# A fourth buffer of H, outputs through lent buffers, and a new written-out order

## The chip, the cores and the metric

The kernel runs on one core of one Trainium2 chip. Such a core has a matrix engine (TensorE, PE in the profile), three engines for elementwise work (VectorE or DVE, ScalarE or ACT, GpSimd or POOL) and a queue (SyncE, SP) from which this kernel issues all its transfers. Each engine runs its own instructions in the order in which they stand in the program, and waits at an instruction until what it needs is there. The metric is the device time of one execution in microseconds; for the kernel before it is the median of three runs.

## The reference

There are four batches of 6272 steps with 256 channels. First a gated recurrence runs along the steps:

```python
sig = 1.0 / (1.0 + np.exp(-f_logit))
f = lower_bound + (1.0 - lower_bound) * sig
i = 1.0 - f
for t in range(S):
    h = f[:, t] * h + i[:, t] * x[:, t]
    y[:, t] = h
```

Its output goes through a projection into three parts of 256 channels. The middle part is convolved, circularly and over all 6272 steps, with a filter for each channel; the result is multiplied by the first and the third part and projected once more:

```python
proj = x @ w_proj                        # x is the y of the recurrence
x1, x2, x3 = the three parts of proj
X2 = np.fft.rfft(x2, n=S, axis=1)
H = np.fft.rfft(filter_fft, n=S, axis=0)[None, :, :]
x2_conv = np.fft.irfft(X2 * H, n=S, axis=1)
out = (x1 * x2_conv * x3) @ w_out
```

## The kernel before

The transform over 6272 = 128 x 49 steps is done as two shorter ones, by matrix products: 128 points, then 49 with a twist (as 98 real rows). The channels are worked in 16 units (`u`) of 16 channels each.

For each batch the steps of the program are these; the words in brackets are the names that the text uses and the lines at which they stand.

- The recurrence (`hgrn`, L318). 13 chunks of 512 steps, the last of 128. For each chunk logits and x are loaded (`load`, L331, 512 KB each), ScalarE takes the sigmoid (`sig`, L334), GpSimd multiplies it with x (`u`, L336), TensorE transposes both (`su`, L348), ScalarE or VectorE makes the gate (`f`, L361 or L363), and VectorE runs the scan (`scan`, L369) into HA. The first 3072 results of each half are repeated behind the last, by GpSimd, ScalarE or a transfer (`wrap`, the helper at L283 to L295).
- The middle projection (`phase_p`, L704). `P` (L713), 13 groups of up to eight products, needs the scan of the whole batch; each group is copied to X2 (`x2`, through the helper, L283 or L288).
- The transform (`phase_f1`, `mini`, `unit`). `F1` (L726) and its copy to A; `F2` (L785); the product with the filter's spectrum H into PP, either by VectorE straight from the matrix engine's results (L806) or by a copy and GpSimd (L815); the way back `I2` (L825) and its copy to Th. H was made once, in a preparation at the start, and lies in HBM; each unit loads its 512 KB (`spectrum_load`, L763) into one of `NH` buffers. The least recently used buffer is taken, and since the units go up in one batch and down in the next, the last `NH` units of a batch find their H in place in the next. With three buffers that makes 55 loads.
- The gate (`gate`, L384): the first and third projections (`x13`, L397) and their product z (L418 by VectorE, L427 by GpSimd).
- The output (`phase_o`, L852). 13 chunks `g`. For each: the second half of the way back (`I1`, L865), needing Th of all units; the product with z into ys (`y`, L871); the output projection (`proj`, L883); the copy of its result into an output buffer (`o`, helper, L285 or L290); the store from there (`store`, L894, 512 KB).

The output buffers are three of their own (`NO = 3`, names `osb`) and four lent ones for chunks 3 to 6: the two buffers PP and two halves of A. A lent buffer is free once the last unit of the batch is done with it, and has to be free again for the first units of the next.

All this is recorded first as a list of steps with what each reads and writes (`Plan.op`), and then issued in the order of a table, `ORDER`, that was made outside of the kernel. An entry names the step, the engine that runs it (where two or three can) and the PSUM bank. The order on each engine and on SP's queue is the table's order, so a later batch's recurrence stands between the earlier batch's steps wherever the table puts it. Each step carries a cost, which only the maker of the table used; transfers carry beside it a `margin` of one microsecond:

```python
op("H", {"SP": 0.46}, lambda e: nc.sync.dma_start(...),
   r=[("H", u, i) for i in range(2)],
   w=[("Hu", h)] + ([("hs", h, a) for a in range(2)] if first else []),
   dma=1.7, lag=2.0, margin=MARGIN)
```

24 groups of four products of no use (`warm`, L599) can stand anywhere; they keep the matrix engine busy.

Of the kernel before, what the change touches and what calls it, by code (L numbers as in the profile page):

```python
# [9 lines left out]
F32 = mybir.dt.float32  # L10
# [14 lines left out]
Q = 49  # L25
# [7 lines left out]
NH = 3  # L33
NO = 3
# [25 lines left out]
class Plan:  # L60
# [63 lines left out]
    "A+gD5gAAYABIACIAsQA0gA5gA1AAyQAgQAuQBDgBNgBXgBIgAhQBSgBhgArQBcgAeQAbQAoQA6ABrgAOYAPIAQAARIAzYA2QA4AA7SA9CA8CBmgA"  # L124
    "/YBAUBBEBCEBwgATIBEYBFWAUIAcSBHGBOYBPSBGGD6gA3ABJYBKUBLEBMMBYYEGgASABTYBRCBQCBZQBaIBbIBiYBUWBWGBjSBlCBkCBdYBeQBg"
    "ABfAAWIBsIBtSBuCBnIBoUBvCAVYAXYAYYAZYAaYBVOAdQBxIBpMByQBzABqMB3SB4KB0AB5QB6ID8AB+UB/MEIAB7YCASCBKD7gD9YCCYCHQESg"
    "EUAEHgB8UCIICDSCECCOWCPGB9MCJQCKIADgAEYD+SD/KEAKEegEgACQUCREECQAFgEDAEEICMWCNGEJYETgCLYCSYCXUAIACYMCZSCaKCeWAHAA"
    "KACTQCfOCUAAGgEfgEKUELMEMMCbYCcSCdCEqgEOWEPGErgCgQEQOEVYChACiYCnSCoCEhYEsACpUCFgCqMCGgE3gE2gCjQCkIEWSEXCEYKEaWEb"
    "GFDgEZgCwUCxEEcOEtYAJACrYCuQGJgCvACyYB1YEiUEjEFCgEmSFMgEnCCzQC0AEkME4AEuWDAUDBECsQCtAEoKEvOEySEzCC+UE5YFNgC5QFEA"
    "FFYEwOFWgALAC/MCVgC6IC3WC4GC7YDCYFXgDDUDEEE0KE6QE7IC8WC9OFOAFPYE8IE+SE/CFggFhgDOUDPEDQWFGUFAKFYAFZYFHEFIMDRGC2gF"  # L130
    "JQFKAFqgAMAE1YFLIDHSDICDJWDKODLYDSYFBYFrgFQUFRMFSMFTSF0gF1gFiAFjYFUCFVKDTQDUADMWDNGDWgFaQFdUF+gDZWFbAFcIFeMFfMF/"
    "gDXSFsAFtYC1gDaGDYCFkWDbYExYDgQF2AFnSF3YEdYEpYFlGFmODeUEFYERYE9YDhAFuQDFgFoCFpKMtgDfEDcWFxUM5gM4gFvAFwIDdGDiYFyE"
    "FzMDpSDqCF4WB2YDjQF5GF6ODkAANACWgF7SGIgCmgDnUMsgF8CDoMDrYDuQGAAGBYF9KEBYJdWJeXJfGDvADwUDxEDyYJgvJiWJkGClgGCQGDIG"
    "EIGFSDsUGGCGHKElYDtEMhgDzWD0GENYMuAMvYD3QGKgD4ID2gGhSGiKGRUGSEGfQGgIGbWGcGGLSGMKMggM6ADlgGPQGQAGjUGkEDVgGTWGUODG"
    "gGZSGaCJjQJloJmYMiAMjYGdUGeMGNSGOCM7YGXQGYAGVUGWMDmgJnSJpKJoTJqrJrYJsQJuAJtRGlUGmEJxQJzIGnWGoGGrSJvpGsKJwYGpUGqE"
    "D1gJyQJ2RJ4BJ0oGwWGtSGuKGyGG5UGvgG0uGzYJ3QJ7RJ5oJ6YJ9BHVSHWCG6YHBgJ1YG1YJ8WKAXKCHJ+uKBRHCSGxYKDBKEYHLWHNGG4gG9sG"
    "+YG7sG8YG2QHGqHKgHDYHECHTVHFYG3AKFSKGUKHCKIsKJYG/QHUFHdgJhYHOYHmgHMYKKSHAIHPuHQYKMCHvgHXTHHYHIVHYDHJFHZQHaAKLSKN"
    "qHeTKPVKQSKRFHirHjYKSCHbQHcIKOYHnWHfYHrGHRUHsYHSEKUSKVXIBQHgrH4gKWCHpuILgHqYKXvKYYICAHoYHhYHkUHlEHwSH0qH1YHyqHzY"
    "HxYIFQIGAIUgKTYIDWHtUKZTKbLH5QIEGHuEIHWIIGH7oH8YH9oH+YH2SIMUIJWIKOH6YKaQH3CIOEIdgKeSIPYKgCINYKcoKfRKhBIQsImgH/TI"
    "VWIWYIXuIRYIADMkQIeSIZGMlAMmIIgCMoUNEgNFgMpEMqMIaYISWITGJ/YIfYKjSKlCIvQIwAIhYIYYI5gIbWIcGInUIoYIiqIjYIrMIsYJCgIx"  # L140
    "QIyAIpsIqYIzSI0CMwWMxOM0QNQgNRgM1AKiYKkUKoVMyONGANHYM2II1SI2CJLgIkWIlGKmsKqFI3SI4KI7YI6QI+oI/YI8AI9YMnYItWIuGJEY"
    "KpSKrqKsYJDUJFEJGYJHsJIYM8QM9ANAWNcgNdgNBGM+IKtSKuTKvCKwrKxYJAUJNYKySNSANTYKzQK3RK0CNCOK1oK2YJBEK5BJMSJQCJRYNIWN"
    "MUJUgNogKdYJJQNpgKnYNJGJOqJPYJWYNNEJKANKONOMK4SK8TNeANfYNUWNYQNygJVUNVGK+DNzgK6qK7YNWOK9SK/qJXEJYYNZALAYLBTNaIJZ"
    "ELDDLCULEsLFYLGWLIGNqANrYMrgLHXLJvLLSLMTNgQNkUN9gLNCLOrLPYLKYJaYNhALQSNlELSCJSWJTGN0AN1YN8gLRTLVSLXCNiILWQLaRNsW"
    "LTrLcBLbTNmMNtGLYoLZYLdrLeYNvUOHgOGgNuOLUYNwENxMJbQJcAR9SR+TSADLkQLlINXYNjYLfWR/CN+ANDYN2UN5SORgOQgLgON6CN7KN/YL"
    "mQN3EN4MLnANPYNbYLogOIAOJYLhWLpSLqKSCQSEALuULvMLiGLjgOAQOBAOCIODSOagObgOECOFKLrWLzULsGL0MLtgOKQL4WOSAOTYMzYNnYOL"
    "AOMILwSL5OLxCLygM/AL1UL9QL+IL2EL3gONSOkgOlgOOCOPKOUWMCUOVGOWOOcAOdYL6QL7AL8gMDML/SMHQMIIMACMBgOXWOYGOZOOeUOhSVMg"
    "VNgOfEOgMM3AOmAOiCOjKMJQMKAMLgMEWOnYOoUOpEOqMOrQVZgVYgMRSOsAOtIVAgMFGMGgVOAMSKMMUVBgNLYOyQOzIO4WO5GPASPBCO8QO9AO"
    "6WO7GMNMPCSPDKVPYO0QO1AO2UO3EVaAVCAVDYOuSPGQPHIOvKO+WO/OPEQPFAOwUOxEMTSMUCMVgMOQMPAMQgPOUMbSMWWPMQPPEPNAMcKPKSVb"
    "YPLCPIUMXOSBYSDWSFGSGYMYQPJMPQSPRKPTYMZAMagPSUPaWPeGPbYPzSP0CSHQSJAPUsPWsPXYPfYSIXSMRSOBSNUSPESQYPcuPdYSKvSLYPrS"  # L150
    "PtCPiQPkAPVYPYUPjYPZEPmoPqgPlYSRSSTCSSQSWWSUoP1UP2EPgRPsYSYOPhBPuYSXQPvqPwYP3WP4GPnYPoUP9gSZoP+RQApQBYQGgQCpQPgP"
    "5WQYgSbQPpEScTP6GSdAPxUPyEP7WP8OP/YSerQHQQLoQMYQJAQDYSgSQIYSiCQhUQiEQEWQFOQQSQUqQVYQSCQKYQZQVEUQrgQTYQ0gQdAQjWVF"
    "EQkGVGMQNRShTSlWQboQcYQOBSjrSkYSnGQlUSmRQeYSopSpYQmEQnWQoGQRYQ9gSqQSrSSsIStqQWUQXEQpQQqIQsWQuuVISQwGQaYVJCSvQVKK"
# [812 lines left out]
```

## Time and profile before

| what | value |
|---|---|
| median of the runs (lowest, highest) | 462.65 us (460.04, 462.97) |
| time of the profiled execution | 464.51 us |
| its span, from the first to the last instruction | 462.3 us |
| mean granted clock of TensorE | 0.989 |
| busy: TensorE / VectorE / ScalarE / GpSimd | 440.1 / 408.1 / 403.6 / 310.3 us |
| moved by transfers | 121.66 MB, mean 263 GB/s |

The profile counts an engine as busy from the start to the end of each of its instructions. A product on TensorE has a modelled end, and starts before the one ahead of it has ended, so its busy time holds some short stops. A row of waits names the waiting engine and line, then who released it, the sum of the time, how many times and the longest.

In this execution the first P starts at about 74 us; what is ahead of it is the preparation and the recurrence of batch 0. P of batch 2 starts at 271 us. The last product ends at about 455.6 us, and what follows is the last copies and stores.

### The profile page before, as it was taken

How to read it: one execution, taken by the hardware profiler on the slowest of the kernel's cores; microseconds unless marked ns; L12 is line 12 of the kernel's file. 1: busy time of each engine (PE TensorE's matmuls, PEld its weight loads, DVE VectorE, ACT ScalarE, POOL GpSimd, SP SyncE). 2: the span in 40 equal slices, each digit the busy share in tenths (PEclk: the TensorE clock that was granted, in tenths of full speed). 3: DMA queues.
4: the chain of work that ended last, by engine and by line, in shares of the span. 5: the costliest groups of instructions: out<-in, count | busy, mean ns of one | idle time of the engine just before them, and what ended most of it. 6: DMA issues, size and time to landing. Idle time of an engine off the chain costs nothing.

```text
span 462.3 us, 14627 instructions
## 1 busy us (share of the span) xinstructions
PE 440.1 (95%) x6009; PEld 347.8 (75%) x6009; DVE 408.1 (88%) x475; ACT 403.6 (87%) x577; POOL 310.3 (67%) x283
## 2 busy tenths in 40 slices
PE   7799889999999999999999999999999899999998
PEld 5677668767767889777668898676768797767787
DVE  8889988799999994899999987999999847999963
ACT  5899898899999989999998988999999778988462
POOL 6978795476999634978997526889986303876400
PEclk9799999999999999999999999999999899999999
DMA  8999999857987995668959983787969822655176
GB/s 323 408 349 336 357 316 339 306 155 214 342 293 253 342 358 181 227 193 272 338 212 331 363 276 145 229 298 262 333 214 300 309 92 84 196 181 183 59 304 255
DMA packets 44530, 121.66 MB, mean 263 GB/s; under 512 B 4272, under 2 KB 6960, under 8 KB 44464
## 3 DMA queue, kind: packets, MB, share of 16 engines
q1 hardware_dynamic: 44464, 120.73, 74.8%
q8 instruction: 47, 0.77, 0.7%
q14 instruction: 19, 0.16, 0.1%
HBM read 87.69 MB, written 31.98 MB: 259 GB/s over the span
## 4 chain that ended last, share of the span: by engine, by line
PE 64%; DVE 11%; ACT 9%; DMA 6%; POOL 5%; issue 4%; SPq 1%; DVEq 0%; POOLq 0%; ACTq 0%
PE PS L397 16%; PE PS L825 8%; PE PS L883 7%; PE PS L713 7%; PE PS L348 7%; PE PS L785 6%; PE PS L726 6%; DVE HA L369 5%; DMA FL<-in_f_logit_dram 3%; PE PS L865 3%; DVE ys L871 3%; POOL XT L336 2%; POOL PP L815 2%; ACT FL L334 2%; ACT fTs L361 1%
## 5 line engine op out<-in xcount | busy, mean ns | idle before, releaser
L336 POOL TENSOR_TENSOR XT<-XT,FL 128x1024 f32<-128x1024 f32 (+1 forms) x49 | 109.8, 2243 | 60.3 <-ACT FL L334 40.9
L369 DVE TENSOR_TENSOR_SCAN HA<-fTs,HA,PS 128x512 f16<-128x512 f32 (+1 forms) x96 | 112.5, 1202 | 6.3 <-ACT fTs L361 5.5
L815 POOL TENSOR_TENSOR PP<-HA,Hu 98x1008 f16<-98x1008 f16 x52 | 109.2, 2107 | 10.0 <-ACT HA L283 8.6
L397 PE MATMUL PS<-HA,W 128*128 128x490 f16 (+1 forms) x416 | 101.5, 367 | 0.8 <-DVE HA L369 0.5
L806 DVE TENSOR_TENSOR PP<-PS,Hu 98x1008 f16<-98x1008 f32 x76 | 89.9, 1200 | 4.2 <-PE PS L785 2.0
L283 ACT CAST HA<-PS 128x1024 f16<-128x1024 f32 (+1 forms) x104 | 83.0, 828 | 3.4 <-PE PS L785 1.5
L871 DVE TENSOR_TENSOR ys<-PS,zt 128x1024 fp32r<-128x1024 f32 (+1 forms) x52 | 58.3, 1151 | 10.6 <-PE PS L865 7.8
L361 ACT ACTIVATE fTs<-PS,nomc 128x512 f32<-128x512 f32 (+1 forms) x93 | 60.3, 669 | 3.0 <-PE PS L348 2.0
L883 PE MATMUL PS<-Wo,ys 128*128 128x256 f32 x392 | 58.5, 296 | 1.2 <-DVE X L288 0.6
L825 PEld LDWEIGHTS <-PP 98*128 98x128 f16 x1024 | 49.5, 98 | 12.4 <-POOL PP L790 2.6
L397 PEld LDWEIGHTS <-W 128*128 128x128 f16 x416 | 35.1, 97 | 29.6 <-issue 5.0
L285 ACT ACTIVATE XS<-PS 128x490 f32<-128x490 f32 (+1 forms) x90 | 51.6, 585 | 6.5 <-PE PS L397 4.3
L283 ACT CAST Th<-PS 128x784 f16<-128x784 f32 x61 | 50.1, 822 | 5.8 <-PE PS L825 4.8
L883 PEld LDWEIGHTS PS<-Wo,ys 128*128 128x128 f32 x392 | 50.5, 192 | 6.2 <-DVE ys L871 1.3
L334 ACT ACTIVATE FL<-FL 128x1024 f32<-128x1024 f32 (+1 forms) x49 | 49.3, 1012 | 6.7 <-DMA FL<-in_f_logit_dram 6.6
L418 DVE TENSOR_TENSOR zt<-PS,XS 128x490 f16<-128x490 f32 (+1 forms) x81 | 51.3, 649 | 3.4 <-PE PS L397 2.1
L825 PE MATMUL PS<-VA,PP 98*128 98x98 f16 x512 | 52.4, 207 | 1.3 <-POOL PP L790 0.8
L825 PE MATMUL PS<-VB,PP 98*128 98x98 f16 x512 | 52.1, 207 | 0.0
L427 POOL TENSOR_TENSOR zt<-XS 128x490 f16<-128x490 f32 x23 | 28.3, 1234 | 28.5 <-DVE ys L871 21.7
L713 PE MATMUL PS<-W,HA 128*128 128x256 f16 x392 | 44.1, 273 | 1.2 <-ACT X L283 0.6
L348 PE MATMUL PS<-iden,FL 64*128 64x64 f32 x736 | 41.9, 230 | 3.0 <-ACT PP L285 1.5
L713 PEld LDWEIGHTS <-HA 128*128 128x128 f16 x392 | 42.9, 142 | 2.1 <-issue 1.6
(117 smaller groups left out, 728.7 us busy)
## 6 DMA issues: line engine op xcount, KB each, us to landing
Hu<-H SPq DMA_DIRECT2D x55, 512.0 KB, 4.4
FL<-in_f_logit_dram SPq DMA_DIRECT2D x45, 512.0 KB, 6.1
XT<-in_x_dram SPq DMA_DIRECT2D x45, 512.0 KB, 6.5
out_dram<-osb SPq DMA_DIRECT2D x32, 512.0 KB, 4.1
X<-in_moe_filter_fft_dram SPq DMA_DIRECT2D x9, 512.0 KB, 7.6
out_dram<-PP SPq DMA_DIRECT2D x8, 512.0 KB, 6.1
out_dram<-HA SPq DMA_DIRECT2D x8, 512.0 KB, 4.4
H<-Hu SPq DMA_DIRECT2D x4, 512.0 KB, 7.5
```

The lines of the kernel that those rows point to most:

```text
L283: nc.scalar.copy(dst, src)
L336: op("u", {"POOL": 0.1 + 0.553 * nb}, lambda e, xt=xt, ft=ft: nc.gpsimd.tensor_tensor(xt, xt, ft, op=AOP.mult), r=[("ft", k)], w=[("xt", k)])
L348: nc.tensor.transpose(bank(pb)[:, at[p] + j:at[p] + hn:nb], src[ps, j, cols], iden[ps, ps])
L361: nc.scalar.activation(fT, sT, AF.Identity, scale=by, bias=1.0)
L369: nc.vector.tensor_tensor_scan(h, fT, bank(pb)[:, 512 - hn:512 + hn], init, op0=AOP.mult, op1=AOP.add),
L397: nc.tensor.matmul(PS[:, p, 0:n], W13[:, kh, js], HA[:, HB[kh] + t0:HB[kh] + t0 + n], start=(kh == 0), stop=(kh == 1))
L713: nc.tensor.matmul(pp[:, r - r0, :], column(HB[kh], q_of(r)), W2[:, kh, :], start=(kh == 0), stop=(kh == 1))
L806: nc.vector.tensor_tensor(pr, px.unsqueeze(1).broadcast_to([TB, 2, UE, 63]), hh, op=AOP.mult)
L815: nc.gpsimd.tensor_tensor(pr, spec[:, o, :, 1:64].unsqueeze(1).broadcast_to([TB, 2, UE, 63]), hh, op=AOP.mult)
L825: nc.tensor.matmul(PS[:, ib + o, pr * TB:(pr + 1) * TB], PP[:TB, k, o, n, 2 * pr:2 * pr + 2, :], v[:TB], start=(n == 0), stop=(n == 1))
L871: nc.vector.tensor_tensor(late["ys"][:, yk, :, 0:rn * 128], PS[:, cb:cb + 2, 0:rn * 128], late["zt"][:].rearrange("p k r m -> p k (r m)") ...
L883: nc.tensor.matmul(po[:, i, :], late["ys"][:, yk, kh, i * 128:(i + 1) * 128], Wo[:, kh, :], start=(kh == 0), stop=(kh == 1))
```

## The change

There are four buffers of H (`NH = 4`). Three (`NK`) lie where the three lay; the fourth lies in the room of the third output buffer, which is gone (`NO = 2`), and can be used only from the end of the preparation on. The units' product with H takes its buffer at the time of issue (`hh` becomes a function). With the same rule for taking a buffer there are 52 loads of H.

Where the output chunks go is now written out in `places`: o0, o1, PP 0, PP 1, A 0, A 1, o0, o1, PP 0, PP 1, o0, o1, o0. So chunks 2, 3, 8 and 9 go through PP and 4 and 5 through A, where before 3 and 4 went through PP and 5 and 6 through A. (`place` knows a further kind, `z`, that the table of places does not use.)

The table `ORDER` is a new one, made without the margins. The steps are the same but for the three loads of H. Some two dozen of the steps that either of two engines can do have changed sides. Thirteen wraps are transfers on SP's queue, where eight were; GpSimd does 26, where it did 32.

```diff
-NH = 3
-NO = 3
+NH = 4
+NK = 3
+NO = 2
...
 ORDER = (
...
-    Hu = konst.tile([128, NH, 2, 2, UE * 64], F16, name="Hu")
+    Hu = konst.tile([128, NK, 2, 2, UE * 64], F16, name="Hu")
...
+    def hu(h):
+
+        return Hu[:, h] if h < NK else late["Hu"][:]
+
     def spectrum_load(u, h):
...
-            Hu[:, h].rearrange("p a e k -> p a (e k)"), turned(H[u // 2][u % 2])),
-           r=[("H", u, i) for i in range(2)],
-           w=[("Hu", h)] + ([("hs", h, a) for a in range(2)] if first else []),
+            hu(h).rearrange("p a e k -> p a (e k)"), turned(H[u // 2][u % 2])),
+           r=[("H", u, i) for i in range(2)] + (["cv"] if h >= NK else []),
+           w=[("Hu", h)] + ([("hs", h, a) for a in range(2)] if first and h < NK else []),
...
-    lend = {3: 0, 4: 1, 5: 2, 6: 3}
+    places = (("o", 0), ("o", 1), ("p", 0), ("p", 1), ("a", 0), ("a", 1), ("o", 0),
+                  ("o", 1), ("p", 0), ("p", 1), ("o", 0), ("o", 1), ("o", 0))
...
-            k = NO + lend[g] if g in lend else count["o"] % NO
-            count["o"] += 1
-            kt = [("osb", k)] + (lent_t[k - NO] if g in lend else [])
+            at, kt = places[g], place_t(*places[g])
...
+            late["Hu"] = cv.tile([128, 2, 2, UE * 64], F16, name="Hl")
             late["Th"] = cv.tile([128, TB, 2, 2, 32], F16, name="Th")
             late["ys"] = cv.tile([128, 2, 2, 512], F32R, name="ys")
             late["osb"] += [cv.tile([128, 4, 256], F32, name=f"osb{i}") for i in range(1, NO)]
```

More of the change, by code (lines that the diff above doesn't have):

```diff
@@ new lines @@
+    "EOEVYEKQCXUEhYAHACeSELAAIAEOWE3gE2gCYMCbYCfCEMIEPGEQOAJACgUCcSChECiYCdCEWQCjUCkEEaWFCgAaYCpSEXIEYIEbGEcOCqCEsACW"
+    "gEiUEjMEtYCmgCnQCoAFDgCrYCwSEkMCuWCxCCvGCyYEmQEnIFMgFNgCzSE4AEoIE5YC0CCsUCtEEuWGJgEZYEvOFEAFFYCFgEySFWgEzKFXgC3Q"
+    "C4AEwOExYC5UC6EE0KALAE6QC7YE7AFOADAUC+WDBMFPYC/GDCYE8IE9YE+SFggE/CFhgFAKC8UC9EAKAFGWFHGDDQDEIDFgFIODHUDIEAMAE1YF"
+    "BYFJSFKCFqgDJQFrgEdYEpgDKIDLYDOUFYAFZYDPEDQWDRGB2YFQQFTUF0gF1gFLKFiADSYDMSDNCDTWDUGFaSFRIC1gFUMFSIFbCDXQDgWDYAFV"
+    "MFcKFjYDZUFdQANADaMDbYDhOFsAF/gFtYFkSFeAFfIDcUFlCFmKDdEF+gDVgFnWMsgMtgF2AClgDeQDfIDnUFoGDoEFpOFuSFvCDjQFwKDkAFxU"
@@ L190 @@
+    "eglgMllKluUlhWliGlmQlnAlvMlpSlzWl4QlwUlxElqKlrSl5Il0OArQAcQlsCAxQl1Ql6SAtUApUAbUAkUAhUAsUAmUljgl2Aloglygl7Cltgl3"
+    "gl8gAyQ"
 )
@@ L922, in turn @@
             late["osb"] += [cv.tile([128, 4, 256], F32, name=f"osb{i}") for i in range(1, NO)]
-            late["osb"] += [v.bitcast(F32).rearrange("p (r e) -> p r e", e=256) for v in lent]
         op("pre", {"SP": 0.01}, turn_head, r=FF1[:NU], w=["cz"])
```

173 lines of the change are left out of this document (92 added, 81 removed).

## The prediction

> **What bounds the kernel now.** I read the page's engine shares first, then the stretches of ten microseconds, then who waits for whom, then the chain that ended last.
>
> ```profile
> span 462.3 us, 14627 instructions
> ...
> PE 440.1 (95%) x6009; PEld 347.8 (75%) x6009; DVE 408.1 (88%) x475; ACT 403.6 (87%) x577; POOL 310.3 (67%) x283
> ...
> PEclk9799999999999999999999999999999899999999
> ```
>
> TensorE is busy for 440.1 of 462.3 us, and VectorE and ScalarE for 88% and 87%. No engine has much room, so an order can win only what stands still: at most 22.2 us of TensorE, and part of that is the start and the last store. The digits under PEclk show a lowered clock in two places, in the second slice and around 365 us. The stretches say how deep the second one is (columns: length, then PE, PEld, DVE, ACT and POOL busy with their counts, clock, DMA share, GB/s):
>
> ```profile
> 270.00:280.00 10.00, 9.79 (x113) 9.62 (x111) 8.04 (x9) 8.65 (x11) 4.79 (x2) 1.00 1.00 362
> ...
> 310.00:320.00 10.00, 9.19 (x146) 6.44 (x144) 9.02 (x12) 9.13 (x15) 9.32 (x9) 1.00 0.89 297
> ...
> 360.00:370.00 10.00, 8.33 (x112) 7.73 (x108) 8.58 (x8) 6.90 (x11) 3.10 (x2) 0.83 0.80 315
> ```
>
> From 360 to 370 TensorE stands 1.67 us and its clock is 0.83, which is 1.7 us of work more: 3.4 us lost, the largest hole after the preparation. From 310 to 320 it stands 0.81 us. Who was waited for, in the whole run and then in the stretch from 345 to 372 us:
>
> ```profile
> POOL XT L336 <- DMA XT<-in_x_dram: 9.0, 4, 6.4
> ...
> ACT FL L334 <- DMA FL<-in_f_logit_dram: 6.6, 7, 1.6
> ...
> PE PS L865 <- ACT HA L285: 1.6, 1, 1.6
> ```
>
> Transfers are waited for by the sigmoid (L334) and by the product after it (L336), that is for the inputs of the scan, x and f_logit. Readers of H (L806, L815) do not wait for transfers at all; their waits are for TensorE and ScalarE:
>
> ```profile
> L815 POOL TENSOR_TENSOR PP<-HA,Hu 98x1008 f16<-98x1008 f16 x52 | 109.2, 2107 | 10.0 <-ACT HA L283 8.6 <-POOL PP L790 0.8 <-POOL zt L427 0.2
> ...
> L806 DVE TENSOR_TENSOR PP<-PS,Hu 98x1008 f16<-98x1008 f32 x76 | 89.9, 1200 | 4.2 <-PE PS L785 2.0 <-PE PS L397 0.8 <-POOL PP L815 0.8
> ```
>
> So the fourth buffer by itself removes no wait that this profile has. What it can do is free SP's queue, in which loads of H stand ahead of other transfers.
>
> **The change part by part**, against the profiled execution's 464.51 us. Which instruction stands where in the new order was read from the two programs' instruction order.
>
> *Work of the engines.* TensorE has the same 762 steps in both. VectorE gets three more copies of A and three more gates f, one more direct product; it loses two Th, two afs and three direct gates.
>
> ```profile
> L418 DVE TENSOR_TENSOR zt<-PS,XS 128x490 f16<-128x490 f32 x73 | 47.1, 659 | 3.1 <-PE PS L397 2.1 <-ACT XS L285 0.2
> ...
> L427 POOL TENSOR_TENSOR zt<-XS 128x490 f16<-128x490 f32 x23 | 28.3, 1234 | 28.5 <-DVE ys L871 21.7 <-ACT XS L283 4.8 <-DVE XS L288 1.9
> ...
> L295 POOL COPY HA<-HA 128x512 f16<-128x512 f16 x32 | 19.0, 613 | 0.0
> ...
> L288 DVE CAST afs<-PS 128x512 fp32r<-128x512 f32 x14 | 9.1, 678 | 1.0 <-issue 0.6 <-PE PS L672 0.4
> ...
> L288 DVE CAST HA<-PS 128x1024 f16<-128x1024 f32 x7 | 8.5, 1222 | 1.8 <-PE PS L726 1.3 <-POOL XT L336 0.5
> ...
> L363 DVE TENSOR_SCALAR fTs<-PS,nomc 128x512 f32<-128x512 f32 x10 | 7.4, 740 | 0.3 <-ACT Th L283 0.2
> ...
> L288 DVE CAST Th<-PS 128x784 f16<-128x784 f32 x3 | 2.9, 964 | 0.0
> ```
>
> 3 x 1.222 + 3 x 0.740 + 1.200 - 2 x 0.964 - 2 x 0.678 - 3 x 0.659 = +1.8 us of 408.1; one or two copies of four further sorts go each way and about cancel. ScalarE gives up what VectorE takes, about as much. GpSimd loses six wrap copies, 6 x 0.613, and one product of 2.107, and gets three gate products of 1.234: about -2. Five of those wraps become transfers on SP's queue, of 128 KB each. VectorE's share is the one that may tell: bounds -1.8 (ScalarE's gain is the one that counts) and +1.8, and I take +0.9.
>
> *H.* 52 loads in place of 55, 1.5 MB of 121.66 less. Nothing waited for them: 0 by itself. The cover is that each load is issued long before its reader.
>
> *The hole around 361 us.* Its rows in the chain that ended last, and SP's queue there:
>
> ```profile
> 305.23 6.46 DMA XT<-in_x_dram
> ...
> 353.67 8.79 DMA FL<-in_f_logit_dram
> ```
> ```profile
> 351.64 0.82 SPq L894 DMA_DIRECT2D out_dram<-osb  x2
> 352.57 1.05 SPq L331 DMA_DIRECT2D XT<-in_x_dram  x1
> 353.67 1.25 SPq L331 DMA_DIRECT2D FL<-in_f_logit_dram  x1
> 355.17 3.39 SPq L894 DMA_DIRECT2D out_dram<-PP  x2
> ```
>
> The logits of chunk 11 of batch 3 are issued at 353.67, after two stores and after that chunk's x, although the sigmoid needs the logits first; they land 8.79 us later, and ScalarE stands 1.6 us. In the new order one of the two stores is behind, and the logits go ahead of x: 1.1 us (353.67 - 352.57) and 512 KB at 315 GB/s, 1.7 us, together 2.8 us earlier than a sigmoid that was 1.6 us late. The hole should close. Bounds -3.4 (all of it) and 0 (another lateness takes its place, the stores below); I take -2.5. Late next is VectorE, which has 8.58 of these 10 us.
>
> *The hole at 310 us.* x of chunk 3 of batch 3, issued at 305.23 behind loads of H, lands at 311.7, and GpSimd's queue, with the step that completes a product for TensorE, stood behind. In the new order this load stands ahead of all but one of that batch's H loads. This is what the fourth buffer gives: -0.8, bounds -0.8 and 0.
>
> *Before the first P.* ScalarE waited 1.39 us for the logits of chunk 1 of batch 1, and TensorE 0.61 us for its copy:
>
> ```profile
> 76.91 1.06 ACT L334 ACTIVATE FL<-FL 128x1024 f32<-128x1024 f32 x1 [1.39 <-DMA FL<-in_f_logit_dram]
> ...
> 82.88 3.65 PE L713 MATMUL PS<-W,HA 128*128 128x256 f16 x32 [0.61 <-ACT X L283]
> ```
>
> The load stood behind three loads and two stores of H; in the new order it is the first of its group: -0.6, bounds -0.6 and 0.
>
> *Fillers.* The 24 groups of four idle matmuls (L599) are the same number. Of those that stand in the stream, not at the start nor behind the last product, there are six in place of two: three in batches 1 and 2, three ahead of the last two products.
>
> ```profile
> 443.04 0.61 PE L599 MATMUL PS<-iden 128*128 128x256 f16 x4
> ```
>
> Four more are 4 x 0.61 = 2.4 us if TensorE is the one waited for, 0 if it would stand there anyway. I take the middle, +1.2.
>
> *Output buffers.* Two of their own in place of three; chunks 2, 3, 8 and 9 go through PP, 4 and 5 through A. A copy into a buffer waits for the store from it, and what is behind that copy on its engine waits too. The rows that price it: median landing of each kind of store, the same for stores from PP in the stretch from 340 to 372, a whole P stage, and one product:
>
> ```profile
> out_dram<-osb SPq DMA_DIRECT2D x32, 512.0 KB, 4.1
> ...
> out_dram<-PP SPq DMA_DIRECT2D x8, 512.0 KB, 6.1
> ```
> ```profile
> out_dram<-PP SPq DMA_DIRECT2D x2, 512.0 KB, 7.7
> ```
> ```profile
> 271.32 10.92 PE L713 MATMUL PS<-W,HA 128*128 128x256 f16 x98
> ...
> 282.00 1.19 PE L883 MATMUL PS<-Wo,ys 128*128 128x256 f32 x8
> ```
>
> In batch 1 the store of chunk 3 now stands on SP's queue behind two loads that wait for the next batch's last transposes, so it is issued about when P of that batch starts; chunk 9 is copied into the same PP buffer after seven of P's 13 groups and its own product: 7 x 10.92 / 12.25 + 1.19 = 7.4 us later. A landing of 6.1 makes it, one of 7.7 does not, by 0.3 us plus SP's issue of 0.4. That copy is on VectorE, and the next copies of x2 (L288), for which P waits, are behind it. In batch 2 chunks 8 and 9 wait likewise for the stores of chunks 2 and 3, and the last gates of the scan are behind them on ScalarE. Bounds 0 and, at 2 us for each of three batches, +6; the nearest row says just late: +1.0.
>
> The Trainium skill, DMA: Bandwidth & Descriptors, section "Anatomy of one DMA — SWDGE (gpsimd) path", gives about 2.0 us plus bytes / 436 GB/s for a transfer, measured on the other kind of queue; for 512 KB that is an estimate of 3.2 us. By it no store would be late, this term would be 0, and the sum 1.0 us lower; the trace's 4.1 to 7.7 us speak against it.
>
> *The end.*
>
> ```profile
> 452.80 1.03 ACT L285 ACTIVATE osb<-PS 128x1024 f32<-128x1024 f32 x1 [0.66 <-PE PS L883]
> ...
> 456.67 0.38 ACT L285 ACTIVATE osb<-PS 128x256 f32<-128x256 f32 x1 [0.21 <-DMA out_dram<-osb]
> ```
>
> Chunk 12 shared its buffer with chunk 9, and waited 0.21 us for the store of it, whose copy had ended at 453.83: 2.84 us. Now it shares with chunk 10, whose copy comes first of the last four. Behind it are the product of chunk 9, the three fillers and the product of chunk 11: 1.19 + 3 x 0.61 + 1.19 = 4.2 us, then the copy of chunk 11. So 2.84 is covered, and 4.1 plus issue nearly: +0.3, bounds 0 and +0.8.
>
> The sum: +0.9 - 2.5 - 0.8 - 0.6 + 1.2 + 1.0 + 0.3 = **-0.5 us**, 464.0 for an execution like the profiled one. That one was 1.86 us over the median of 462.65, so **462.1** for the median.
>
> **The rivals.**
>
> *A, the holes close and nothing opens.* Every term at its low end: -1.8 - 3.4 - 0.8 - 0.6 = -6.6, so 456.0. For it: the three late loads all stand earlier now. Against it: TensorE's 95%.
>
> *B, slower: stores hold up copies at the turn of a batch.* If the stores from PP land in 8 us or more there, as they did between 340 and 372 within 0.3 us, the copy of chunk 8 or 9 stands, and with it x2 or the last gates, and then P. A stop of 1.6 us (the row of L865 above) was followed by the lowered clock, which cost 1.7; so 2.0 + 1.7 = 3.7 us for each turn of a batch. Two turns in place of the +1.0: 462.1 - 1.0 + 7.4 = 468.5; three 472.2. It decides from a landing of about 8 us. For it: the transfer engines are at 1.00 in the stretch 270 to 280 us. Against it: 3 H loads less, and in batches 0 and 3 the distances are longer.
>
> The Trainium skill, TensorE: Matmul & The Clock Gate, section "Part 1: The HAM clock gate", has the clock fall after an idle window of about 3.4 us. By that rule stops of 2 us would not bring it down, and B would cost 2.0 for a turn, 465.1 with two; the trace shows it down after a longest stop of 1.6 us.
>
> *C, the change does not do what it says.* H is loaded earlier, nobody waited for H, and the loads of x and logits stay late in the same places, since transfers of the same size share the same engines: the three gains are 0, and the sum +3.4: 466.0.
>
> **How the numbers follow.** A measurement of this kernel can tell about 1% from no change, 458.0 to 467.3. Forecast 0.31, C 0.14: both within, 0.45. A 0.26: faster. B 0.29: slower. The range 456 to 470 holds the forecast, C, A down to its price and the milder half of B; about 0.1 is left out on each side.
>
> **What would show it.** The wait of the sigmoid for its logits, 6.6 us before, falls below 4, and the stretch at the turn into batch 3 has clock 1.00. No reader of H waits for a transfer. GpSimd's idle time before L336 put down to the transfer of x falls. If B is right, copies of the output (ScalarE or VectorE) show waits for out_dram of over 1 us at the turns, against 0.2 in all before. Wrong I would be above all through holes that neither order's text shows: waits among the engines that come from the new order itself, worth more than the three that close.

## The result, and the profile after

The changed kernel takes 457.69 us (median; 455.85 to 458.23), beside 462.97 us (460.04 to 465.8) of the kernel before: 0.990 of it, 95% interval 0.986 to 0.993. Measured a second time, on one of the chips of the experiments below, it took 457.33 us and 0.988 (0.984 to 0.992). So it is faster by about 1.1%, some 5 us: inside the predicted range, 4.4 us below the forecast of 462.1, and close to the price of rival A, 456.0. The profiled execution took 457.45 us. The ratios here and below leave out executions that were over 1.5% above the fastest of their kernel, and are not the quotients of the medians beside them.

The page of the changed kernel, the lines that answer to those of before:

```profile
span 455.6 us, 14635 instructions
...
PE 439.6 (96%) x6009; PEld 348.4 (76%) x6009; DVE 407.4 (89%) x476; ACT 402.3 (88%) x577; POOL 308.8 (68%) x279
...
PEclk9599999999999999999999999999999999999999
```

The span is 6.7 us shorter, while TensorE is busy for 0.5 us less: the engines do the same work and stand still less. The lowered clock around 365 us is gone; the one at the start is longer, 10.2 us in place of 6.8. VectorE is busy 0.7 us less, not more.

Stretches of the changed kernel, with the columns of the stretches above (length, PE, PEld, DVE, ACT, POOL, clock, DMA share, GB/s):

```profile
310.00:320.00 10.00, 10.00 (x153) 7.53 (x152) 9.83 (x13) 9.73 (x16) 10.00 (x9) 1.00 0.87 321
...
360.00:370.00 10.00, 9.29 (x137) 8.59 (x132) 8.87 (x10) 6.58 (x10) 1.85 (x2) 1.00 0.55 214
```

The hole at 310 us is closed (9.19 before, 10.00 now), and the turn into batch 3 has full clock. Waits of the changed kernel (engine, line, released by: sum, times, longest):

```profile
POOL XT L337 <- DMA XT<-in_x_dram: 11.8, 3, 7.0
...
ACT FL L335 <- DMA FL<-in_f_logit_dram: 0.6, 1, 0.6
...
ACT osb L286 <- DMA out_dram<-osb: 0.3, 1, 0.3
```

The sigmoid's wait for its logits fell from 6.6 to 0.6 us. GpSimd's wait for x did not fall (9.0 to 11.8). Copies of the output wait 0.3 us in all for a store. The issues of the stores (count, KB each, median us to landing):

```profile
out_dram<-osb SPq DMA_DIRECT2D x24, 512.0 KB, 4.6
...
out_dram<-PP SPq DMA_DIRECT2D x16, 512.0 KB, 4.8
```

Where the 6.7 us are is best read from stretches that end where P of a batch starts, so: preparation with the recurrence of batch 0; three stretches from P to the next batch's P; the last, from P of batch 3 to the end of the last product; and what comes behind it. Before:

```profile
0.00:74.31 74.31, 63.82 (x691) 50.09 (x692) 66.94 (x100) 64.98 (x98) 60.92 (x84) 0.95 0.96 344
74.31:170.16 95.85, 93.45 (x1372) 72.39 (x1371) 89.91 (x99) 88.77 (x127) 68.57 (x54) 1.00 0.83 287
170.16:271.32 101.16, 98.50 (x1443) 78.01 (x1441) 91.38 (x100) 93.42 (x134) 72.10 (x56) 1.00 0.77 265
271.32:372.35 101.03, 97.40 (x1426) 78.13 (x1423) 90.97 (x99) 93.43 (x136) 72.87 (x55) 0.98 0.76 259
372.35:455.58 83.23, 82.11 (x1047) 65.04 (x1045) 68.95 (x80) 61.76 (x85) 35.81 (x34) 1.00 0.49 172
455.58:462.30 6.72, 4.82 (x45) 4.08 (x42) 0.00 (x0) 1.26 (x2) 0.00 (x0) 1.00 0.52 200
```

After:

```profile
0.00:71.51 71.51, 64.15 (x687) 50.71 (x688) 66.13 (x101) 64.06 (x99) 60.39 (x83) 0.93 0.98 364
71.51:167.07 95.56, 93.76 (x1374) 72.72 (x1373) 88.46 (x97) 91.05 (x132) 70.86 (x54) 1.00 0.84 281
167.07:265.99 98.92, 96.49 (x1421) 77.15 (x1418) 92.59 (x101) 90.26 (x131) 68.46 (x53) 1.00 0.74 260
265.99:366.02 100.03, 98.49 (x1453) 78.73 (x1451) 91.83 (x103) 93.36 (x132) 73.00 (x55) 1.00 0.76 268
366.02:450.37 84.35, 83.19 (x1055) 66.15 (x1053) 68.37 (x79) 62.36 (x86) 36.06 (x34) 1.00 0.49 169
450.37:455.50 5.13, 3.51 (x33) 2.90 (x30) 0.00 (x0) 1.22 (x2) 0.00 (x0) 1.00 0.49 192
```

The third and fourth rows must be read together, because the new order does 22 products fewer in the third and 27 more in the fourth. Together they last 202.2 us before and 198.9 after, 3.3 less: TensorE stood 6.3 us of it before (2.66 + 3.63) and 4.0 after (2.43 + 1.54), and the lowered clock had cost 1.7; against that stand 0.8 us more of work. The first row is 2.8 shorter. The last two also belong together, since idle matmuls moved from behind the last product to ahead of it: 89.95 before, 89.5 after.

### The profile page after: what moved, and what is told of

It is laid out like the page before. It is cut to its first block, busy times and chain, and to the rows that moved or that the text cites. A ratio compares the mean times of both kernels' runs of the same rounds, so it can differ in the third digit from the quotient of the medians.

```text
span 455.6 us, 14635 instructions
## 1 busy us (share of the span) xinstructions
PE 439.6 (96%) x6009; PEld 348.4 (76%) x6009; DVE 407.4 (89%) x476; ACT 402.3 (88%) x577; POOL 308.8 (68%) x279
## 4 chain that ended last, share of the span: by engine, by line
PE 72%; DVE 11%; ACT 9%; issue 4%; DMA 3%; POOL 1%; SPq 0%; ACTq 0%; DVEq 0%; POOLq 0%
PE PS L398 17%; PE PS L714 9%; PE PS L832 9%; PE PS L913 8%; PE PS L790 7%; DVE HA L370 7%; PE PS L727 6%; PE PS L349 6%; PE PS L895 4%; ACT fTs L362 2%; DMA X<-in_moe_filter_fft_dram 2%; PE PS L600 2%; ACT HA L284 2%; DVE ys L901 1%; ACT X L284 1%
## 5 line engine op out<-in xcount | busy, mean ns | idle before, releaser
L398 PE MATMUL PS<-HA,W 128*128 128x490 f16 (+1 forms) x416 | 100.2, 367 | 0.3 <-ACT Th L284 0.2
L822 POOL TENSOR_TENSOR PP<-HA,Hu 98x1008 f16<-98x1008 f16 x42 | 88.0, 2106 | 5.6 <-ACT HA L284 2.6
L284 ACT CAST HA<-PS 128x1024 f16<-128x1024 f32 (+1 forms) x101 | 81.2, 831 | 3.3 <-POOL PP L822 0.8
L813 DVE TENSOR_TENSOR PP<-PS,Hu 98x1008 f16<-98x1008 f32 x54 | 63.6, 1199 | 1.5 <-PE PS L790 0.7
L428 POOL TENSOR_TENSOR zt<-XS 128x490 f16<-128x490 f32 (+1 forms) x26 | 31.8, 1223 | 39.0 <-DVE ys L901 27.4
L913 PE MATMUL PS<-Wo,ys 128*128 128x256 f32 x392 | 57.5, 293 | 0.4 <-DVE ys L901 0.3
L284 ACT CAST Th<-PS 128x784 f16<-128x784 f32 x63 | 52.0, 828 | 3.4 <-PE PS L832 2.7
L419 DVE TENSOR_TENSOR zt<-PS,XS 128x490 f16<-128x490 f32 (+1 forms) x78 | 49.2, 648 | 2.7 <-ACT XS L286 0.8
```

Source lines behind the costliest of these rows:

```text
L284: nc.scalar.copy(dst, src)
L398: nc.tensor.matmul(PS[:, p, 0:n], W13[:, kh, js], HA[:, HB[kh] + t0:HB[kh] + t0 + n], start=(kh == 0), stop=(kh == 1))
L813: nc.vector.tensor_tensor(pr, px.unsqueeze(1).broadcast_to([TB, 2, UE, 63]), hh(), op=AOP.mult)
L822: nc.gpsimd.tensor_tensor(pr, spec[:, o, :, 1:64].unsqueeze(1).broadcast_to([TB, 2, UE, 63]), hh(), op=AOP.mult)
L913: nc.tensor.matmul(po[:, i, :], late["ys"][:, yk, kh, i * 128:(i + 1) * 128], Wo[:, kh, :], start=(kh == 0), stop=(kh == 1))
```

## The experiments

The changed kernel was measured again beside some of them.

> The changed kernel itself, beside the others on one chip. Its first measurement gave 0.990 of before. If the gain is real, it comes out at 0.987 to 0.993 here, 1.000 would say that the first result was scatter. It is also the measure for the kernel with six fillers moved (0.998): if the changed kernel stays at 0.990, the fillers in the stream cost nothing and may even help by 3 us; if it comes out at 0.997, the two are equal.

0.988: the first result holds. It stays below the kernel with six fillers moved, for which a reason is found with the fillers below.

Three things were open: whether the gain is the order of the loads, the fourth buffer, or the rest of the new order; whether what one profile of before showed is there in every execution; and why the stores did not hold anything up. All times are beside runs of the kernel before on the same chip.

| kernel | median, us (lowest to highest) | before, us | ratio (95%) |
|---|---|---|---|
| new buffers, old order | 459.41 (457.88 to 461.63) | 461.44 | 0.997 (0.994 to 1.000) |
| new order, three buffers of H | 466.55 (461.46 to 470.85) | 461.44 | 1.009 (1.005 to 1.013) |
| before, late loads early | 458.89 (457.76 to 460.64) | 461.44 | 0.997 (0.994 to 1.000) |
| changed, six fillers behind the end | 459.84 (458.02 to 461.19) | 461.44 | 0.998 (0.996 to 1.001) |
| changed, again | 457.33 (455.77 to 459.39) | 462.29 | 0.988 (0.984 to 0.992) |
| before, new preparation, fillers ahead of P | 462.84 (461.07 to 465.36) | 462.29 | 1.002 (0.999 to 1.006) |
| the same, late loads early | 462.35 (461.19 to 463.38) | 462.29 | 0.998 (0.995 to 1.001) |
| spliced | 468.82 (466.30 to 471.33) | 462.29 | 1.012 (1.008 to 1.017) |
| before, new preparation alone | 459.83 (458.37 to 465.13) | 461.69 | 0.998 (0.995 to 1.001) |
| changed, no fillers behind the end | 458.43 (456.87 to 460.56) | 461.69 | 0.994 (0.992 to 0.996) |
| changed, fillers at the start only | 458.24 (456.55 to 459.84) | 461.69 | 0.993 (0.990 to 0.995) |
| before, again | 461.89 (458.39 to 465.11) | 461.69 | 1.001 (0.997 to 1.004) |

The stages of one profiled execution of each, in us, read from the starts of P as above:

| kernel | to first P | batch 0 | batches 1 and 2 | last product and end |
|---|---|---|---|---|
| before | 74.3 | 95.9 | 202.2 | 90.0 |
| before, again | 72.6 | 96.9 | 200.1 | 89.7 |
| before, new preparation alone | 71.4 | 95.4 | 201.8 | 89.9 |
| before, late loads early | 73.8 | 95.3 | 198.8 | 90.2 |
| before, new preparation, fillers ahead of P | 77.3 | 95.4 | 199.4 | 89.0 |
| the same, late loads early | 76.5 | 95.7 | 199.8 | 89.5 |
| new buffers, old order | 71.8 | 96.0 | 198.1 | 90.0 |
| new order, three buffers | 71.5 | 96.5 | 203.9 | 92.0 |
| spliced | 71.4 | 95.6 | 205.7 | 91.3 |
| changed | 71.5 | 95.6 | 198.9 | 89.5 |
| changed, again | 71.9 | 96.2 | 197.9 | 89.5 |
| changed, six fillers behind the end | 73.0 | 95.8 | 197.7 | 91.7 |
| changed, no fillers behind the end | 72.2 | 95.6 | 197.8 | 89.6 |
| changed, fillers at the start only | 71.3 | 95.5 | 198.3 | 89.5 |

### New buffers with the old order

The changed kernel's code, with the table of before; the three loads of H that four buffers save are left out of it, and one step of batch 2 is put off until its buffer is free.

```diff
 NH = 4
 NO = 2
-ORDER = (the new table)
+ORDER = (the table of before, less three loads of H)
```

> The buffers of the changed kernel (four of H, two own output buffers, chunks 2, 3, 8, 9 through PP) with the order of the kernel before; three loads of H are left out of its order and one step is put off until its buffer is free. Theory (late loads of x and logits, which the new order issues earlier): the loads stand where they stood, so 461 to 465, and the sigmoid waits for its logits for about 6 us in all. Rival 1 (the fourth buffer of H itself): about 458. Rival 2 (the new order as a whole, stage by stage): 461 to 465 as well.

0.997: 459.41 us, between the theory's 461 to 465 and the 458 of rival 1, and the sigmoid waits 4.0 us, not 6. By the ratios about three quarters of the gain are not in the buffers and the places alone. Its profile has batches 1 and 2 at 198.1 us, as short as the changed kernel's. But a copy of the output at the end waits longer (waits of this kernel):

```profile
ACT FL L332 <- DMA FL<-in_f_logit_dram: 4.0, 5, 1.3
...
ACT osb L283 <- DMA out_dram<-osb: 2.9, 1, 2.9
```

With two output buffers and the old order of the chunks, the copy of the last chunk waits 2.9 us for the store of an earlier one; the new order has changed that sequence. The last stretch is no longer for it than that of before (90.0 us both), 0.5 us longer than the changed kernel's. The profiled execution was, at 457.91, near the fastest of this kernel, so its stages flatter it.

### The new order with three buffers of H

```diff
-NH = 4
+NH = 3
 ORDER = (
...
+    three loads of H more, and 27 steps later than in the table, where a buffer comes free later
```

> The new order and output places with three buffers of H: 55 loads of H, each put off until its buffer is free, 27 of them later than in the new order. Theory (late loads): the loads of x and logits keep their places relative to the compute steps, but stand behind more waiting loads of H; some wait comes back, 458 to 461. Rival 1 (the fourth buffer): 462 or more, with waits for H on VectorE or GpSimd. Rival 2 (the order as a whole): 457.5 to 458.5.

1.009, where the changed kernel is at 0.988 to 0.990, with waits for H as rival 1 had them: the new order needs its fourth buffer, and is worth 2% less without it. Waits of this kernel in the stretch from 267 us to the end:

```profile
POOL XT L334 <- DMA XT<-in_x_dram: 13.4, 3, 8.2
ACT FL L332 <- DMA FL<-in_f_logit_dram: 5.0, 2, 3.9
POOL PP L819 <- DMA Hu<-H: 3.7, 3, 1.3
DVE PP L810 <- DMA Hu<-H: 2.1, 1, 2.1
```

Readers of H, which waited for no transfer in the first profile of before, now do, 5.8 us in this stretch (3.7 + 2.1), and the late logits are back, once by 3.9 us. A load of H that comes when its buffer is free, not when the queue has room, is late itself and makes others late.

### The late loads early, and nothing else

Three places in the order of SP's queue; the names are of the transfers, with their chunk and batch.

```diff
+logits, chunk 1, batch 1
 x, chunk 1, batch 1
...
-logits, chunk 1, batch 1
...
 logits, chunk 3, batch 3
+x, chunk 3, batch 3
 H, unit 4, batch 2
...
-x, chunk 3, batch 3
...
 store, chunk 1, batch 2
+logits, chunk 11, batch 3
+x, chunk 11, batch 3
 store, chunk 2, batch 2
-x, chunk 11, batch 3
-logits, chunk 11, batch 3
```

> The kernel before with three changes on SP's queue alone: logits of chunk 11 of batch 3 ahead of that chunk's x and of one store, x of chunk 3 of batch 3 ahead of the loads of H, logits of chunk 1 of batch 1 ahead of its neighbours. Theory (late loads): the three holes close, 3.9 us less, 458.5 to 460, clock 1.00 between 355 and 370 us. Rival 2 (the order as a whole): the waits go and the time stays, 462 to 464.

0.997: a gain of 0.3%, 1.4 us, with an interval of 0 to 2.9; by the medians it is 2.6. The time is within the theory's 458.5 to 460. The two later holes are closed in its profile, and batches 1 and 2 last 198.8 us. So the prediction's mechanism is there, and gives between a third and two thirds of what it was priced at (2.5 + 0.8 + 0.6 = 3.9). One reason why it is less shows in the next run.

### The kernel before, once more

> The kernel before, once more with a profile. If its hole at the turn into batch 3 is what the trace showed, the stretch of ten microseconds there has a clock under 1.00 and the sigmoid waits over 4 us for logits again, and the third stage is 101 us long (98.0 with the loads early). If the wide scatter of this kernel (457 to 466) comes from that hole, its runs' mean clocks go with their times; if all clocks are alike, it doesn't.

Stretches of this execution of the kernel before, then its waits:

```profile
310.00:320.00 10.00, 10.00 (x160) 7.15 (x157) 9.71 (x13) 9.62 (x16) 9.64 (x9) 1.00 0.87 300
...
360.00:370.00 10.00, 9.32 (x159) 8.42 (x156) 9.87 (x11) 9.09 (x14) 3.12 (x2) 1.00 0.74 288
```
```profile
ACT FL L334 <- DMA FL<-in_f_logit_dram: 4.7, 6, 2.2
```

The same program, and both holes on which the prediction rested are gone: 10.00 in place of 9.19 and 9.32 in place of 8.33, clock 1.00 in place of 0.83. Batches 1 and 2 last 200.1 us in place of 202.2. The sigmoid waits 4.7 us all the same, at other loads; the loads on its chain of waits are others:

```profile
48.72 6.22 DMA FL<-in_f_logit_dram
68.83 7.12 DMA FL<-in_f_logit_dram
214.40 5.84 DMA Hu<-H
255.13 9.22 DMA XT<-in_x_dram
293.44 5.67 DMA FL<-in_f_logit_dram
```

In the first profile they were, after 100 us, x at 305 and logits at 353. One of those here is a load of H (214.40), for which VectorE waited 0.9 us; in the first profile no reader of H waited. So the kernel before has many loads that are nearly late, and which of them is too late changes from one execution to the next; a hole read in one profile costs its full size only in the executions that have it. The clocks go with the times: the six runs with a mean clock of 1.00 average 460.4 us, the six below it 463.1. That may be some of the scatter of this kernel (458.4 to 465.1 here); with the three loads early it is 457.8 to 460.6. Where the clock was lowered in the runs without a profile is not known, and in the changed kernel's second measurement the runs with a lowered clock are not the slower ones.

### The preparation

Before, with the preparation's order of the changed kernel. In a first form eight groups of idle matmuls (fillers) had come to stand right ahead of the first P:

```diff
 ORDER = (
-    390 entries up to the first P, as before
+    the entries of the new table up to the first P
+    eight groups of fillers
...
```

> Before, with only the order of the preparation (everything up to the first P of batch 0) taken from the changed kernel. Theory 1, the preparation's own order gives its 2.8 us (first P at 71.5 in place of 74.3): 0.994. Rival, the start of the first P scatters by some 2 us from one execution to the next whatever the order (the kernel with the old order and the new buffers had 71.8): 1.000, between 0.998 and 1.002.

1.002. This does not show the preparation's order alone. TensorE's timeline of this kernel:

```profile
73.80 3.65 PE L596 MATMUL PS<-iden 128*128 128x256 f16 x32 [0.83 <-DVE Hu L287]
77.29 0.93 PE L710 MATMUL PS<-W,HA 128*128 128x256 f16 x7
```

P started behind 32 idle matmuls at 77.3. The kernel without them there, below, is at 459.83, 3 us lower (2 by the ratios). The same with the loads of batch 3 early as well:

```diff
 the kernel above
+x, chunk 3, batch 3 and the two loads of chunk 11, batch 3, where the previous diff has them
```

> Before, with the preparation's order of the changed kernel and the two late groups of loads of batch 3 (logits and x of chunk 11, x of chunk 3) issued earlier; three buffers of H, outputs where they were. If the gains of preparation and of the early loads add: 0.994 times 0.997 = 0.991, so the whole gain without the fourth buffer. If the preparation gives nothing: 0.997.

0.998: 0.4% below the kernel above by the ratios, which is about what the early loads give by themselves (0.3%), but only 0.5 us by the medians. The expectation that the two gains add, 0.991, was not met; with the fillers ahead of P this kernel could not show it. Then the new preparation alone, with the fillers at the start and where before has them:

```diff
 ORDER = (
-    390 entries up to the first P, as before
+    the entries of the new table up to the first P
...
```

> Before, with the preparation's order of the changed kernel and nothing else; the idle matmuls stand at the start and where before has them (in the kernel with the new preparation tried earlier, eight groups of them had come to stand right ahead of the first P, and it started at 77.3). Theory: the order of the preparation gives at most 1 us, since the kernel with the old order and the new buffers also started P at 71.8; first P at 72 to 74.5, ratio 0.996 to 1.000. Rival: the order of the preparation gives the 2.8 us; first P below 72 and 0.994.

0.998 (0.995 to 1.001), about 1 us (1.9 by the medians), as the theory had it, though P started at 71.4, where the rival had it. The eight profiles with the new preparation (those with fillers ahead of P left out) start P at 71.3 to 73.0, mean 71.8; the four with the old at 71.8 to 74.3, mean 73.1. The 2.8 us between the first two profiles are half scatter.

### The fillers

The changed kernel has three groups in batches 1 and 2 and three ahead of the last two products; all six moved behind the last product:

```diff
 ORDER = (
...
-    filler (batch 1), filler, filler (batch 2)
...
-    filler, filler, filler
     the last two products
+    six fillers
     eight fillers
```

> The changed kernel with its six groups of idle products that stand in the stream put behind the last product. Theory: the three ahead of the last two products cost TensorE 1.3 us at the end, the others nothing to 1.1: 455.3 to 457. Rival: they keep the clock up, so that without them it falls somewhere, 458 to 460.

0.998, where 455.3 to 457 us had been expected: 459.84, no gain over the changed kernel. The stream got 1.1 us shorter (377.8 from first P to last product, in place of 378.9) and the end 2.1 longer. Stretches of one microsecond of this kernel's end:

```profile
454.00:455.00 1.00, 1.00 (x11) 0.89 (x10) 0.00 (x0) 0.00 (x0) 0.00 (x0) 1.00 0.43 148
455.00:456.00 1.00, 1.00 (x12) 0.89 (x10) 0.00 (x0) 0.00 (x0) 0.00 (x0) 1.00 0.00 0
456.00:457.00 1.00, 0.91 (x9) 0.57 (x6) 0.00 (x0) 0.00 (x0) 0.00 (x0) 1.00 0.00 0
```

The last transfer is over before 455; then only idle matmuls run, for two more microseconds. In the changed kernel (the same view) fillers and stores end together, between 453 and 454:

```profile
453.00:454.00 1.00, 0.88 (x9) 0.54 (x6) 0.00 (x0) 0.00 (x0) 0.00 (x0) 1.00 0.73 266
454.00:455.00 1.00, 0.00 (x0) 0.00 (x0) 0.00 (x0) 0.00 (x0) 0.00 (x0) 1.00 0.00 0
```

To see which of the two sets the end there, the eight behind the last product were left out, and then the six in the stream too. Fillers are no part of the result.

```diff
-WARM = 24
+WARM = 16
 ORDER = (
...
-    eight fillers behind the last product
```

> The changed kernel without the eight groups of idle matmuls behind the last product (32 matmuls, 3.5 us; they are no part of the result). Theory 1, the chain of waits is right that they set the end: 3.5 us less, 0.980. Theory 2, the last store lands at the same time (transfers ran until 453.7, the idle matmuls until 453.9): at most 0.3 us less, 0.987.

```diff
-WARM = 24
+WARM = 10
 ORDER = (
...
-    six fillers in the stream, eight behind the last product
```

> The changed kernel with the ten groups of idle matmuls at the start and no others: neither the six in the stream nor the eight behind the last product. The kernel that had the six moved behind the last product was 1.1 us shorter from the first P to the last product (377.8 in place of 378.9) and 2.1 longer behind it. If the six cost that 1.1 us and serve nothing: 1.1 to 1.4 us below the changed kernel, 0.985. If stops of TensorE that they fill bring the lowered clock: at or above the changed kernel, 0.988 to 0.995, with a lowered clock in the middle.

0.994 and 0.993: neither below the changed kernel. Without the last eight, what follows the last product is 5.2 us as before (449.94 to 455.13), though the chain of waits of the changed kernel had named them as what ended last; the store ends with them and holds the end just as well. Theory 2 holds on the length of the end; the ratio came out above both expectations. Both kernels lie some 0.8 us above the changed one, which was measured beside others; whether that is more than scatter is open. What the six in the stream cost is within the scatter too: from the first P to the last product the three profiles with them take 377.8, 378.5 and 378.9 us, the two without 377.8 and 378.2. Without them the clock was not lowered between the preparation and the last product, so the rival that they keep it up is not borne out.

### The spliced order

The changed kernel up to the first P of batch 2, from there the order of before with the late loads early; the three fillers in batches 1 and 2 are left out.

```diff
 ORDER = (
     the new table up to the first P of batch 2
-    the rest of the new table
+    the rest of the table of before, late loads early
```

> The changed kernel up to the first P of batch 2, and from there the order of before with the late loads of batch 3 early, and the three fillers ahead of the last two products as in the changed kernel; no fillers in batches 1 and 2. If each stage keeps the length that it had in the kernel it comes from: 71.5 + 95.6 + 98.9 + 98.0 + 83.5 + 5.2 = 452.7 us of span, 454.6 us, 0.985. Rival, a stage's length is set by what the stage before it has left over (fillers and steps that are pulled forward), so that the splice gives back what it wins: 0.990 or more.

1.012, where the sum of the best stages would be 0.985 and the rival had 0.990 or more: 11 us slower than the changed kernel. The joint changed the turn of batch 1 into batch 2. Stretches and timeline of this kernel there:

```profile
264.00:267.00 3.00, 1.41 (x36) 1.15 (x36) 2.86 (x5) 2.10 (x5) 0.46 (x1) 0.98 0.92 314
267.00:270.00 3.00, 2.35 (x16) 2.13 (x18) 0.59 (x1) 0.00 (x0) 0.00 (x0) 0.50 0.91 257
270.00:273.00 3.00, 0.69 (x14) 0.56 (x9) 1.22 (x1) 0.00 (x0) 0.00 (x0) 0.50 1.02 418
```
```profile
264.30 1.19 PE L892 MATMUL PS<-ID,Th 64*128 64x128 f16 x32
...
265.33 0.38 SPq L922 DMA_DIRECT2D out_dram<-PP  x1
...
267.65 2.08 PE L910 MATMUL PS<-Wo,ys 128*128 128x256 f32 x8 [2.15 <-DVE ys L898]
...
273.01 1.02 ACT L283 ACTIVATE PP<-PS 128x1024 f32<-128x1024 f32 x1 [6.75 <-DMA out_dram<-PP]
274.09 1.22 PE L711 MATMUL PS<-W,HA 128*128 128x256 f16 x5 [3.40 <-ACT PP L283]
```

The joint put chunk 9's product (L910, at 267.65) and its copy ahead of P, where the changed kernel has seven groups of P before them. So TensorE had no P to fill in with while it waited 2.15 us for VectorE's ys, and the clock went to half in that stop, at 266.9, before any store held anything up. Then comes what rival B describes: the store of chunk 3 from PP is issued at 265.33 and lands 7.7 us later, the copy of chunk 9 into that buffer stands on ScalarE for 6.75 us, 3.3 of them after its product had ended, and TensorE stands for 3.40. B's condition was another, a landing of 8 us or more; here the copy had come too near to the store.

The stage is 107.1 us long, where the changed kernel's is 98.9, but it also holds that product and the I1 of chunk 11, which the changed kernel does behind the first P. Batches 1 and 2 together, with the same steps but for three fillers, are 6.8 us longer (205.7 - 198.9).

The changed kernel has the same store at the same time, with the copy behind it in another place (its timeline):

```profile
265.90 0.38 SPq L925 DMA_DIRECT2D out_dram<-PP  x1
...
273.53 1.22 DVE L291 TENSOR_SCALAR PP<-PS 128x1024 f32<-128x1024 f32 x1
```

7.6 us from the one to the other, and no wait in this execution. In the kernel with the fillers at the start only, which has the same order there, the copy did wait (its timeline):

```profile
265.52 0.46 SPq L922 DMA_DIRECT2D out_dram<-PP  x1
...
273.48 1.22 DVE L288 TENSOR_SCALAR PP<-PS 128x1024 f32<-128x1024 f32 x1 [0.25 <-DMA out_dram<-PP]
```

The store landed 8.0 us after its issue (273.48 - 265.52), and the copy was 0.25 us early. So the changed order passes this point with nothing to spare.

## Why the prediction was right or wrong

It forecast 462.1, inside the 1% that it called no change, and gave 0.26 to faster by more; the time came out 4.4 us lower, just past that 1%, and within the range. Against its sum of -0.5 us stand about -5. That the range held it says little for the sum, and that it lies near A's 456.0 does not bear A out: A has the three holes at 4.8 us, and moving just those loads gave 1.4 (0 to 2.9), so this nearness is luck as far as the runs show. Term by term:

- **Engines, +0.9: wrong.** The step took VectorE's instruction counts by their mean durations, +1.8, and charged half. Those groups did grow, by 1.7 us, but the sorts of copies that it let cancel fell by 0.3, and small steps of the preparation, the same in both kernels, by 0.9. So all of VectorE's durations together grew by 0.4; they overlap, and its busy time fell by 0.7. ScalarE is busy 1.3 less, and TensorE stands less than before.
- **The holes at 361 and 310 us and ahead of the first P, -2.5, -0.8, -0.6: right in mechanism, wrong as a price for the median.** In the changed kernel's profile they are closed. But the second profile of before has neither of the first two, and moving just these loads gives 1.4 us (0 to 2.9; 2.6 by the medians), not 3.9. The first profile was an execution with a hole.
- **"The fourth buffer by itself removes no wait ... free SP's queue": half right.** In the profile that the step read no reader of H waited, and with the old order the new buffers give 0.3% (0 to 0.6). But that was one execution: in six profiles with the order of before, or near it, and three buffers the readers of H wait 0, 0, 0.9, 1.7, 2.4 and 2.6 us in all, in the seven with four buffers 0 in six and 0.4 in one. So the buffer does remove a wait, a small one. And the new order is built on it: without the buffer that order has waits for H of 7.2 us in the whole run, and is slower than before by 0.9%. Rival C, that the loads stay late, is refuted by the sigmoid's wait, 6.6 to 0.6 (1.8 in the second profile of the changed kernel).
- **Fillers, +1.2: too high, as far as the runs can tell.** The profiles with and without the six in the stream overlap, and the time without them is not lower. The term went by the length of a filler; that most stand where TensorE would have stood anyway is likely, but not shown.
- **Output buffers, +1.0: the working was right, the size was not.** It put the copy of chunk 9 7.4 us behind the issue of chunk 3's store; measured, 7.6. It feared a landing of up to 7.7; in the spliced order it was 7.7, in another profile 8.0. The cost was nothing in the first profile of the changed kernel and 0.25 us in that other. The estimate from the Trainium skill (DMA: Bandwidth & Descriptors, section "Anatomy of one DMA — SWDGE (gpsimd) path"), 3.2 us for 512 KB, had this term at 0 as well. The landings here are 4.6 and 4.8 us by the median and 7.7 to 8.0 at this place, so it gave the right term for a wrong reason.
- **Rival B** did not happen, and its mechanism is real. Its point of decision, a landing of about 8 us, was right: one of 8.0 made a copy wait, by 0.25 us. Its price, 3.7 us for a turn, was not measured by itself. In the spliced order the store made TensorE stand for 3.40 us, where B had 2.0, but the clock had fallen before that, in a stop of 2.15 us that no store made, so the 6.8 us of batches 1 and 2 are the price of both. The rule quoted in B from the Trainium skill (TensorE: Matmul & The Clock Gate, section "Part 1: The HAM clock gate") has the clock fall after an idle window of about 3.4 us. In the spliced trace it fell 1.4 us into that stop, against the rule, as it fell in the trace of before.
- **The end, +0.3: small, with the wrong sign.** From P of batch 3 to the end it is 0.4 us shorter. The part behind the last product fell from 6.7 to 5.2: three groups of fillers stand ahead of it now (TensorE busy for 4.8 us behind it before, 3.5 after), and the transfers end about as much sooner after it. Which of the two did it is not shown.
- **What the prediction had no term for** is the rest of the order. It is a larger change than the text ahead of the prediction has it: over 200 steps run on another engine than before, and some two dozen is only what the counts differ by. By the ratios the preparation gives about 1 us, the early loads 1.4; those two and the end make about 2.8 of 5. By the medians (1.9 and 2.6) they would make nearly all of it, and the kernel that could decide, before with the new preparation and the early loads but no fillers ahead of P, was not measured. Batches 1 and 2 are at 197.7 to 198.9 us in all five profiles of the changed order with four buffers, at 198.1 with the old order and four buffers, and at 198.8 and 199.8 in the two of before with early loads, against 199.4 to 202.2 in four of before without. So the cause of the remaining 2 us stays open; the intervals of the parts are nearly as wide.
- **GpSimd's wait for x** was to fall and rose from 9.0 to 11.8. It is harmless: GpSimd is busy 68% of the span, and has 1% of the chain that ended last.

## What to carry to other kernels

A hole in one profile is a sample: before it is priced, look at a second execution, and count how many transfers land close to their reader. An order that gives all of them room seems to win by it, and scatters less here: 455.8 to 459.4 us in the changed kernel's two measurements, 458.4 to 465.1 in one of before. An order and its buffers are one thing; the table made for four buffers loses 2% with three, and half of one table joined to half of another made TensorE stand for 2.15 and 3.40 us where the changed kernel does not. Where a copy reuses a buffer, note the distance from the store's issue to the copy beside the landing measured at that place, not the median: here 7.6 against 7.7 to 8.0.

## What was not expected of the hardware

A lowered clock for 10.2 us in the preparation cost nothing that shows. The changed kernel's second profile has none there, and its first row reads:

```profile
0.00:71.86 71.86, 61.31 (x688) 47.84 (x688) 66.03 (x101) 64.51 (x99) 60.66 (x83) 1.00 0.98 362
```

With the lowered clock (0.93) TensorE was busy 64.15 of 71.51 us, without it 61.31 of 71.86: in both the transfers have a share of 0.98, and P starts at nearly the same time (71.5 and 71.9).

The clock also falls sooner than a long stop would explain. In the spliced order it was at half from 266.9 us, 1.4 us into a stop. Behind the last product of the kernel without fillers behind the end, which ended at 449.94, TensorE had nothing left, and the clock stayed at 1.00 for 2.7 us more. So the length of the stop does not decide.

But for those that the end cuts off, the lowered stretches last 3.41 us, or two or three times that, and the two of the kernel before begin 351.6 us apart, which is 103 times 3.41. Stretches of 3.41 us that are laid so that one ends where the clock falls read as follows (the kernel before, twice; the spliced order; the kernel without fillers behind the end):

```profile
362.76:366.17 3.41, 1.76 (x46) 1.38 (x46) 2.02 (x2) 3.41 (x5) 2.36 (x1) 1.00 0.72 280
366.17:369.58 3.41, 3.41 (x34) 3.29 (x33) 3.41 (x4) 1.92 (x5) 0.74 (x1) 0.50 0.81 314
```
```profile
263.47:266.88 3.41, 1.62 (x40) 1.23 (x38) 3.27 (x5) 2.63 (x6) 0.99 (x2) 1.00 0.92 322
```
```profile
449.25:452.66 3.41, 0.69 (x6) 0.48 (x5) 0.00 (x0) 1.41 (x2) 0.00 (x0) 1.00 0.73 293
```

TensorE was busy for 52%, 48% and 20% of the stretch that ends with the fall. Ten of the profiles have such falls within the span, 14 in all, and the stretch ahead of each is busy for 20 to 61%. No stretch of this grid with more is followed by a fall, and a few of 52 to 61% are not either. This would fit a clock that is set anew every 3.41 us by the share of the time in which TensorE was busy. It is read off these profiles, and no run was made to test it.
